# A gated linear recurrence and a gated linear unit on one core: another hand-written order of all queues, other PSUM banks, four groups of unread matmuls in place of eleven

## The chip, the cores and the metric

The kernel runs on one core of a Trainium2 chip. The metric is the device time of one execution in microseconds. All input and output tensors lie in HBM; the kernel is launched once.

## The reference

The input x has 4 sequences of 6336 steps with 256 channels, as have the two gates. A recurrence along time is computed for each channel, then a causal convolution of 5 taps whose sigmoid gates a linear map, then a second linear map.

```python
a_base = sigmoid(a_param)                        # 256 channels
log_a  = 8.0 * sigmoid(r_gate) * log(clip(a_base, 1e-6, 1 - 1e-6))
a_t    = exp(log_a)
x_gated = sqrt(maximum(1 - a_t * a_t, 1e-6)) * sigmoid(i_gate) * x
for t in range(S):
    h = a_t[:, t] * h + x_gated[:, t]
    y[:, t] = h
gate = sigmoid(causal_conv(y, conv_w))           # 5 taps, one set for each channel
out  = (gate * (y @ w_val)) @ w_out              # two 256 x 256 matrices
```

## The kernel before

The 25344 time steps (4 x 6336) are cut into 51 windows: two of 256 steps, 48 of 512 and a last one of 256. Windows are grouped into 28 chunks: chunks 0, 1, 2, 26 and 27 hold one window (0, 1, 2, 49 and 50), every other chunk holds two. Chunk 3 is windows 3 and 4, chunk 7 windows 11 and 12, chunk 16 windows 29 and 30, chunk 24 windows 45 and 46. The sequence boundaries fall inside chunks. All intermediate tensors live in rings of buffers that the work goes round: 4 windows each for r, i and x as they are loaded, 4 for the output, 3 for the gate, 5 chunks for a, 10 windows for u.

The program takes no decision at run time or by a scheduler. A text, `ORDER`, lists words, and a loop at L530 emits the instructions of each word in that order. Every engine takes its own instructions strictly in the order of the text, so the text fixes the queue of each engine and of SP, which issues all large DMAs. A word names an operation, its window or chunk, sometimes a half of the channels (0 or 1), and behind `@` the PSUM banks (of eight) that it writes. The framework adds semaphores where one instruction needs another's result or the buffer that it still reads. The operations of one window or chunk, in the order in which data passes through them:

| word | engine, line | what it does |
|---|---|---|
| `lr`, `li`, `lx` (window) | SP, L290 | loads 512 KB of r, i or x (256 KB for a short window) |
| `ta`, `tb` (chunk) | ACT, L308, L311 | tanh of r/2 and of i/2 (the sigmoids) |
| `tr` (chunk, half) | PE, L355 | transposes the tanh of r into PSUM, 16 matmuls for a pair of chunks |
| `ex` (chunk, half) | ACT, L376 | exp: a, for one chunk or a pair |
| `sq`, `sa` (chunk, half) | POOL, L384; ACT, L392 | a squared |
| `rt` (batch) | ACT, L403 | square root of 1 - a squared, for two or three chunks at once, with another activation table |
| `nt` (chunk) | PE, L418 | transposes the root back |
| `pp`, `up` (window) | POOL, L318, L330 | 1 + tanh, then times x |
| `xp`, `uv` (window) | PE, L335; DVE, L344 | the same product for windows 1, 2 and 6, with x passed through PSUM |
| `xg` (chunk) | DVE, L425 | times the root: the recurrence's input u |
| `xt` (chunk) | PE, L434 | transposes u |
| `sc` (chunk, half) | DVE, L456 | the scan along time |
| `cv` (window) | PE, L468 | the convolution, 20 matmuls with diagonal weights |
| `tg` (window) | ACT, L475 | tanh of half the convolution (the gate) |
| `vl` (window) | PE, L483 | y times w_val |
| `gv` (window) | DVE, L488 | (1 + gate) times val |
| `ou` (window) | PE, L498 | times w_out |
| `cd`, `ca` (window) | DVE, L506; ACT, L508 | copies the result out of PSUM |
| `st` (window) | SP, L519 | stores 512 KB |
| `wm` (number) | PE, L362 | five 128x512 matmuls of an identity into a bank that nobody reads |

The words `s_wl.0` to `s_wl.3` load the two weight matrices and `s_wcast` converts them on POOL. The loop at L530 puts in an activation table load (1.28 us each in the trace, at L535) whenever ACT goes from tanh or exp to the square root or back, so a run of `rt` costs two.

A load waits for the operation that frees its slot, and everything behind it in SP's queue waits too; a store waits for its copy in the same way. Words on PE wait likewise for the reader of the bank that they are going to write: `vl.44@2,3` waits for `tg.43`, for instance, where `cv.43` was the last to write banks 2 and 3.

```python
for word in ORDER.split():
    word, _, at = word.partition("@")
    name, *idx = word.split(".")
    if table.get(name, have) != have:
        have = table[name]
        nc.scalar.preload_act_table_set(have)
    emit[name](*[int(k) for k in idx], *[int(k) for k in at.split(",") if k])
```

Of the kernel before, what the change touches and what calls it, by code (L numbers as in the profile page):

```python
# [53 lines left out]
gv.9 st.7 cv.10@4,5 li.20 ta.12 li.18 sc.7.0 pp.16 li.17 vl.8@0,1 sq.10.0 vl.10@6,7 tg.10 lr.26 li.19 gv.8
ou.9.0@4,5 pp.13 gv.10 wm.2@2 ou.8.0@0,1 rt.5 up.14 cd.9.0 ou.10.0@6,7 tr.11.1@2 sc.7.1 st.9 up.16 lr.25 cd.10.0
cv.11@4,5 up.13 cd.8.0 st.10 nt.8@6,7 lr.23 tr.11.0@3 st.8 pp.15 xg.8 tg.11 vl.11@0,1 lr.24 lx.18 ex.11.1 up.15
xt.8@6,7 gv.11 lx.17 ex.11.0 nt.9@4,5 sc.8.0 sq.11.1 tb.10 cv.12@0,1 tr.12.0@3 xg.9 ex.12.0 li.22 pp.17 li.21 sc.8.1
tg.12 pp.18 ou.11.0@4,5 tb.11 xt.9@2,3 sq.11.0 vl.12@0,1 cd.11.0 cv.13@6,7 ta.14 sq.12.0 gv.12 st.11 li.23 cv.14@4,5
tg.13 sc.9.1 lr.29 pp.20 ou.12.0@0,1 ta.13 up.18 vl.13@6,7 cd.12.0 tr.12.1@3 tg.14 up.17 sc.9.0 st.12 tr.13.1@0,1
ex.12.1 lx.19 lx.20 nt.10@4,5 ex.13.1 li.24 sq.12.1 gv.13 tr.13.0@2,3 tb.12 xg.10 ou.13.0@6,7 sq.13.1 xt.10@4,5  # L60
cd.13.0 ex.13.0 cv.15@0,1 pp.22 sc.10.0 st.13 lx.21 cv.16@6,7 pp.19 lx.22 tg.15 lr.28 lr.30 sq.13.0 vl.15@2,3 tg.16
sc.10.1 li.25 vl.14@0,1 lr.27 pp.21 vl.16@6,7 gv.15 rt.6 sq.14.1 gv.14 ou.15.0@2,3 up.19 gv.16 cv.17@4,5 ou.14.0@0,1
cd.15.0 up.20 ou.16.0@6,7 cd.14.0 st.15 li.26 nt.11@2,3 cd.16.0 sq.14.0 lx.24 vl.17@0,1 tg.17 xg.11 st.14 lx.23
tb.13 st.16 gv.17 xt.11@2,3 up.21 cv.18@4,5 sc.11.1 sc.11.0 li.27 nt.12@0,1 li.28 ta.15 up.22 vl.18@6,7 tg.18 lr.32
pp.23 lr.31 ta.16 ou.17.0@4,5 pp.24 gv.18 up.24 tb.14 xg.12 tr.15.1@2,3 cv.20@6,7 cd.17.0 ex.15.1 xt.12@0,1 up.23
# [501 lines left out]
```

## Time and profile before

| what | before |
|---|---|
| device time, median of 3 runs | 290.36 us (290.32 to 290.96) |
| device time of the profiled execution | 290.72 us |
| its span, first to last instruction | 288.6 us |
| instructions in the span | 6363 |
| mean granted TensorE clock | 0.996 |
| moved by DMA | 104.76 MB, mean 363 GB/s |
| POOL products (L330) | 48, 100.9 us busy |
| DVE scans (L456) | 54, 105.8 us busy |
| PE convolutions (L468) | 1080 matmuls, 62.9 us busy |
| PE unread matmuls (L362) | 55, 14.0 us busy |

Times inside the span are counted from its start, in microseconds. Rows of the timeline give start and duration of instructions merged by line and shape, and in brackets the idle time of the engine before them and what ended it; rows of the waits give the total, the number and the longest of such waits. In the text, the time of a word is that of its instructions in the trace, found by counting through `ORDER` engine by engine.

### The profile page before, as it was taken

How to read it: one execution, taken by the hardware profiler on the slowest of the kernel's cores; microseconds unless marked ns; L12 is line 12 of the kernel's file. 1: busy time of each engine (PE TensorE's matmuls, PEld its weight loads, DVE VectorE, ACT ScalarE, POOL GpSimd, SP SyncE). 2: the span in 40 equal slices, each digit the busy share in tenths (PEclk: the TensorE clock that was granted, in tenths of full speed). 3: DMA queues.
4: the chain of work that ended last, by engine and by line, in shares of the span. 5: the costliest groups of instructions: out<-in, count | busy, mean ns of one | idle time of the engine just before them, and what ended most of it. 6: DMA issues, size and time to landing. Idle time of an engine off the chain costs nothing.

```text
span 288.6 us, 6363 instructions
## 1 busy us (share of the span) xinstructions
PE 250.6 (87%) x2552; PEld 169.4 (59%) x2552; DVE 247.0 (86%) x214; ACT 273.7 (95%) x197; POOL 241.5 (84%) x161
## 2 busy tenths in 40 slices
PE   2397799879898899889898999889799897999993
PEld 1253557547656677466567585467457664676552
DVE  5002899869999999999998999989999999999891
ACT  4999999999999999999999999999999999999754
POOL 1669469999999999999999999999998999496100
PEclk9999999999999999999999999999999999999998
DMA  7999999999999999999999999999999999885554
GB/s 240 396 392 409 407 374 385 357 385 371 403 407 410 410 395 366 375 346 417 418 408 341 376 413 414 418 395 396 351 352 412 420 386 408 263 292 208 199 221 182
DMA packets 29996, 104.76 MB, mean 363 GB/s; under 512 B 3335, under 2 KB 3854, under 8 KB 29966
## 3 DMA queue, kind: packets, MB, share of 16 engines
q1 hardware_dynamic: 29952, 104.35, 93.9%
q8 instruction: 20, 0.33, 0.5%
q14 instruction: 10, 0.08, 0.1%
q10 hardware_dynamic: 14, 0.01, 0.0%
HBM read 78.39 MB, written 25.95 MB: 362 GB/s over the span
## 4 chain that ended last, share of the span: by engine, by line
POOL 31%; PE 20%; DMA 15%; DVE 12%; ACT 12%; issue 7%; SPq 2%; DVEq 0%; ACTq 0%; POOLq 0%
POOL uring L330 14%; POOL ering L384 11%; DMA xring<-in_x_dram 8%; POOL tbring L318 6%; PE banks L468 6%; DMA iring<-in_i_gate_dram 6%; DVE yring L456 5%; DVE tgring L488 4%; PE banks L483 4%; PE banks L498 3%; PE banks L418 3%; ACT aring L376 3%; ACT tbring L311 3%; ACT ering L403 2%; SPq L290 2%
## 5 line engine op out<-in xcount | busy, mean ns | idle before, releaser
L330 POOL TENSOR_TENSOR uring<-tbring,xring 128x1024 bf16<-128x1024 bf16 (+1 forms) x48 | 100.9, 2116 | 11.1 <-DMA xring<-in_x_dram 10.6
L456 DVE TENSOR_TENSOR_SCAN yring<-aring,yring,banks 128x1024 bf16<-128x1024 f32 (+5 forms) x54 | 105.8, 1987 | 0.2
L384 POOL TENSOR_TENSOR ering<-aring 128x1024 f32<-128x1024 f32 (+2 forms) x54 | 91.7, 1715 | 14.7 <-ACT aring L376 14.6
L468 PE MATMUL banks<-yring,diag 64*64 64x512 bf16 (+7 forms) x1080 | 62.9, 361 | 4.6 <-DVE yring L456 3.6
L488 DVE SCALAR_TENSOR_TENSOR tgring<-tgring,banks 128x1024 bf16<-128x1024 bf16 (+1 forms) x51 | 59.3, 1178 | 5.1 <-PE banks L483 2.4
L498 PE MATMUL banks<-wo,tgring 128*128 128x256 bf16 x396 | 51.1, 274 | 7.5 <-DVE tgring L488 4.9
L376 ACT ACTIVATE aring<-banks,khf 128x2048 f32<-128x2048 bf16 (+3 forms) x38 | 53.9, 1467 | 0.4 <-PE banks L355 0.4
L475 ACT ACTIVATE tgring<-banks 128x1024 bf16<-128x1024 f32 (+1 forms) x51 | 50.5, 1007 | 3.0 <-PE banks L468 2.9
L318 POOL TENSOR_SCALAR tbring<-tbring 128x1024 bf16<-128x1024 bf16 (+1 forms) x48 | 49.0, 1030 | 4.4 <-ACT tbring L311 4.3
L498 PEld LDWEIGHTS <-tgring 128*128 128x128 bf16 x396 | 41.4, 114 | 18.6 <-DVE tgring L488 10.5
L483 PE MATMUL banks<-yring,wv 128*128 128x512 bf16 (+4 forms) x216 | 49.6, 361 | 1.6 <-ACT aring L376 0.8
L308 ACT ACTIVATE taring<-rring 128x2048 bf16<-128x2048 f32 (+2 forms) x28 | 47.6, 1718 | 2.4 <-DMA rring<-in_r_gate_dram 2.4
L311 ACT ACTIVATE tbring<-iring 128x2048 bf16<-128x2048 f32 (+2 forms) x28 | 47.9, 1719 | 0.0
L468 PEld LDWEIGHTS <-diag 64*64 64x64 bf16 x1080 | 29.1, 106 | 28.1 <-issue 11.6
L403 ACT ACTIVATE ering<-ering 128x4096 bf16<-128x4096 f32 (+5 forms) x15 | 44.7, 3016 | 0.1
L506 DVE COPY oring<-banks 128x1024 f32<-128x1024 f32 (+1 forms) x36 | 42.0, 1182 | 1.6 <-PE banks L498 1.1
L355 PE MATMUL banks<-ident_b,taring 128*128 128x128 bf16 x396 | 30.2, 230 | 9.4 <-ACT taring L308 7.2
L425 DVE TENSOR_TENSOR uring<-banks,uring 128x2048 bf16<-128x2048 bf16 (+2 forms) x28 | 30.4, 1093 | 6.7 <-PE banks L418 5.7
L355 PEld LDWEIGHTS <-taring 128*128 128x128 bf16 x396 | 26.1, 103 | 15.1 <-ACT taring L308 9.2
L483 PEld LDWEIGHTS <-wv 128*128 128x128 bf16 x216 | 19.9, 98 | 21.3 <-issue 7.1
L418 PE MATMUL banks<-ident,ering 128*128 128x128 f32 x198 | 29.7, 292 | 1.9 <-DVE yring L456 0.9
L418 PEld LDWEIGHTS banks<-ident,ering 128*128 128x128 f32 x198 | 25.9, 207 | 9.1 <-ACT ering L403 3.5
(45 smaller groups left out, 139.7 us busy)
## 6 DMA issues: line engine op xcount, KB each, us to landing
rring<-in_r_gate_dram SPq DMA_DIRECT2D x48, 512.0 KB, 7.9
iring<-in_i_gate_dram SPq DMA_DIRECT2D x48, 512.0 KB, 8.2
xring<-in_x_dram SPq DMA_DIRECT2D x48, 512.0 KB, 7.9
out_dram<-oring SPq DMA_DIRECT2D x48, 512.0 KB, 5.8
rring<-in_r_gate_dram SPq DMA_DIRECT2D x3, 256.0 KB, 4.4
iring<-in_i_gate_dram SPq DMA_DIRECT2D x3, 256.0 KB, 5.8
xring<-in_x_dram SPq DMA_DIRECT2D x3, 256.0 KB, 8.2
out_dram<-oring SPq DMA_DIRECT2D x3, 256.0 KB, 7.4
```

Of the source, the lines that this page charges most:

```text
L311: nc.scalar.activation(**tangent(c, tbring, NTI, iring, NII))
L318: nc.gpsimd.tensor_scalar(out=t, in0=t, scalar1=1.0, scalar2=1.0, op0=ALU.mult, op1=ALU.add)
L330: nc.gpsimd.tensor_tensor(out=u, in0=t1, in1=xt, op=ALU.mult)
L355: nc.tensor.transpose(out=bank[:, o:o + P], in_=taring[:, place(w, NTR), j, h * P:(h + 1) * P], identity=ident_b[:])
L376: nc.scalar.activation(out=dst, in_=src, func=ACT.Exp, scale=khf[:, h:h + 1], bias=khf[:, h:h + 1])
L384: nc.gpsimd.tensor_tensor(out=e, in0=a, in1=a, op=ALU.mult)
L418: nc.tensor.transpose(out=bank[:, k:k + P], in_=ering[:, e + q:e + wins[w] // 2:nq], identity=ident[:])
L456: nc.vector.tensor_tensor_scan(out=yring[:, h, col:col + o1 - o0], data0=aring[:, h, a_at[c] + o0:a_at[c] + o1], data1=xT[:, o0:o1], initi ...
L468: nc.tensor.matmul(out=gp[oh * 64:oh * 64 + 64, h, a:b], lhsT=diag[half * 64:half * 64 + 64, h, k, :], rhs=yring[half * 64:half * 64 + 64, ...
L483: nc.tensor.matmul(out=val[:, m, a:b], lhsT=wv[:, hk, m * P:(m + 1) * P], rhs=yring[:, hk, col:col + b - a], start=(hk == 0), stop=(hk == ...
L488: nc.vector.scalar_tensor_tensor(out=tgring[:, w % NTG, :, 0:wins[w]], in0=tgring[:, w % NTG, :, 0:wins[w]], scalar=1.0, in1=live.pop(("va ...
L498: nc.tensor.matmul(out=ops[:, j * D:(j + 1) * D], lhsT=gv[:, hk, j:wins[w]:J], rhs=wo[:, hk, :], start=(hk == 0), stop=(hk == H - 1))
```

## The change

Only the text `ORDER` is replaced; every function, ring, chunk and group of chunks stays as it was, and so do all line numbers. Both texts hold the same words except these: there are 11 `wm` words before and 4 after; and the copies of windows 5, 23, 34 and 39 go from ACT to DVE (`ca` to `cd`), those of windows 16, 29, 33 and 36 from DVE to ACT. The words stand in another order for every engine and for SP, and most PE words write other banks. The number of switches between activation tables is 18 in both.

In the head and around the places that are spoken of below, the diff reads:

```diff
 ORDER = """
-s_ident s_small s_kt s_diag lr.2 lr.0 s_wl.3 lr.1 li.0 lr.3 s_wl.2 ta.2 ta.0 lr.4 tr.0.1@0 ta.1 lr.6 tr.2.0@1 tb.0
-lr.5 tr.1.0@2 tr.0.0@3 tr.2.1@4 ex.2.0 li.1 tr.1.1@5 li.2 ex.1.1 li.3 ex.0.1 sq.1.1 lx.0 ex.1.0 li.4 sq.2.0 ex.0.0
-ex.2.1 sq.1.0 ta.3 sq.2.1 pp.0 sq.0.0 ta.4 sq.0.1 tb.1 lr.10 tr.3.0@4,5 tb.2 lr.9 lr.8 tr.3.1@2,3 lr.7 ex.3.0 lx.2
-s_wl.1 up.0 lx.1 ex.3.1 sq.3.0 lx.4 lx.3 wm.10@6 tb.3 sq.3.1 ta.6 pp.4 wm.5@6 wm.3@6 wm.9@6 wm.6@6 sq.4.1 lr.13 ta.5
...
-gv.9 st.7 cv.10@4,5 li.20 ta.12 li.18 sc.7.0 pp.16 li.17 vl.8@0,1 sq.10.0 vl.10@6,7 tg.10 lr.26 li.19 gv.8
...
-xt.8@6,7 gv.11 lx.17 ex.11.0 nt.9@4,5 sc.8.0 sq.11.1 tb.10 cv.12@0,1 tr.12.0@3 xg.9 ex.12.0 li.22 pp.17 li.21 sc.8.1
...
-sc.13.0 ou.19.0@4,5 pp.25 cd.19.0 up.25 wm.16@6 sc.13.1 st.19 li.32 nt.14@4,5 up.27 lx.29 li.31 ta.18 lr.36 lx.30
...
-xg.16 li.35 xt.15@4,5 sq.18.0 ca.23.0 gv.24 cv.26@2,3 li.36 ta.20 sc.15.0 sq.17.0 cv.25@6,7 st.22 tg.26 tr.19.0@0,1
...
-tr.25.1@0 up.42 ex.25.1 nt.22@4,5 cd.35.0 tg.38 ou.36.0@0,1 sq.24.0 xg.22 sa.25.1 st.35 tr.25.0@6 lr.50 vl.38@2,3
...
-vl.41@2,3 xg.24 ta.26 tr.27.0@6 xt.23@0,1 gv.41 ex.27.0 ou.39.0@4,5 tb.25 sc.23.0 cv.42@2,3 ca.39.0 ou.41.0@6,7
...
-sc.24.0 tr.27.1@7 ca.40.0 cv.44@0,1 ex.27.1 up.47 st.40 cv.43@2,3 ex.26.1 lx.49 sc.24.1 tg.44 sa.27.1 nt.25@6,7
-sq.26.1 tg.43 vl.42@0,1 sq.27.0 tb.26 xg.25 vl.44@2,3 sq.26.0 tb.27 vl.43@4,5 gv.42 pp.50 xt.25@6,7 pp.49 gv.44
-ou.42.0@0,1 rt.11 gv.43 ou.44.0@2,3 up.49 ca.42.0 sc.25.1 ou.43.0@4,5 ca.44.0 st.42 cv.45@0,1 ca.43.0 st.44
...
+s_ident s_small s_kt s_diag lr.0 s_wl.2 ta.0 lr.2 li.0 ta.2 tr.2.0@0 tr.0.1@1 lr.1 lr.3 lr.4 ta.1 lr.6 tb.0 lr.5
+ex.0.1 tr.1.1@2 ex.1.1 ex.2.0 tr.2.1@3 tr.1.0@4 ex.1.0 li.1 li.2 li.4 ex.2.1 ta.3 wm.6@5 tr.0.0@4 sq.2.0 ta.4 lx.0
+wm.9@5 li.3 lr.7 lr.10 lr.9 tr.3.1@2,3 tr.3.0@0,1 lx.1 lr.8 sq.2.1 pp.0 up.0 sq.1.0 ex.0.0 sq.0.0 lx.2 lx.3 xp.1@4
+s_wl.3 tb.2 lx.4 tb.1 ex.3.1 li.5 sq.3.1 lx.5 uv.1 s_wl.1 sq.0.1 sq.1.1 ex.3.0 tb.3 wm.11@5 ta.6 xp.2@4,5 ta.5 lr.13
+s_wl.0 rt.0 nt.0@0 sq.3.0 rt.2 rt.1 nt.2@1 uv.2 pp.4 sq.4.1 sq.4.0 xg.0 up.4 pp.3 xg.2 nt.1@2 xt.0@4,5 li.6 xg.1
+xt.1@2,3 tr.5.1@0,1 sc.0.0 up.3 s_wcast rt.3 sc.0.1 ex.5.1 nt.3@4,5 sc.1.1 sc.1.0 xg.3 cv.0@6,7 tg.0 lr.11 li.8
+xt.2@2,3 lr.14 li.7 lx.6 lr.12 sc.2.1 sc.2.0 cv.1@4,5 sq.6.1 vl.1@0,1 tr.5.0@6,7 vl.0@2,3 tg.1 tb.4 gv.1 gv.0
...
+nt.8@0,1 sc.7.0 cv.12@4,5 cd.8.0 xg.8 vl.12@6,7 tr.11.1@2 st.8 tg.12 lr.26 ex.11.1 ex.11.0 gv.12 xt.8@0,1 cv.11@4,5
...
+sc.14.0 cv.23@0,1 li.31 li.32 ou.22.0@2,3 cd.22.0 lx.30 ex.17.1 tb.16 nt.15@6,7 st.22 cv.25@4,5 lx.29 xg.15 ta.19
...
+pp.41 up.40 li.45 li.46 ex.23.1 sq.24.0 pp.42 xg.21 ou.34.0@2,3 xt.21@6,7 cv.37@0,1 gv.35 cd.34.0 ta.25 tr.25.1@2
...
+ex.26.1 cv.44@2,3 sc.24.1 sc.24.0 ex.27.0 ou.42.0@0,1 ex.27.1 tb.26 sq.26.0 pp.47 sq.27.0 sq.26.1 up.47 tg.44
+sa.27.1 ca.42.0 cv.43@6,7 tg.43 nt.25@2,3 xg.25 pp.49 st.41 st.40 vl.43@0,1 vl.44@6,7 st.42 gv.44 lx.49 li.50 lx.50
...
 """
```

More of the change, by code (lines that the diff above doesn't have):

```diff
@@ new lines @@
+ou.1.0@0 ou.0.0@1 ex.5.0 xt.3@2,3 cd.1.0 st.1 cd.0.0 ta.8 cv.2@4,5 tg.2 li.10 pp.5 st.0 sc.3.0 sc.3.1 vl.2@6,7
+xp.6@0,1 nt.4@4,5 ta.7 gv.2 uv.6 lx.7 up.5 lx.9 li.9 tb.5 lx.8 lr.15 tr.7.0@2,3 lr.17 tr.7.1@6,7 xg.4 ou.2.0@0,1
+sq.5.0 ex.7.0 xt.4@4,5 cd.2.0 sq.5.1 sq.6.0 sq.7.0 pp.7 sc.4.1 st.2 sc.4.0 ex.7.1 li.12 lr.16 tb.6 cv.3@2,3 cv.4@0,1
+tg.4 lr.18 li.14 lx.10 vl.4@6,7 gv.4 vl.3@0,1 tg.3 gv.3 sq.8.0 sq.7.1 rt.4 ou.4.0@6,7 pp.9 cd.4.0 cv.5@2,3
+ou.3.0@0,1 cv.6@6,7 cd.3.0 pp.8 up.8 up.7 tg.6 st.4 li.11 st.3 nt.5@0,1 tg.5 ta.9 vl.6@4,5 li.13 lx.11 lx.12 xg.5
@@ new lines @@
+lr.19 lr.20 gv.6 xt.5@0,1 sq.8.1 up.9 ta.10 vl.5@2,3 ou.6.0@4,5 nt.6@6,7 pp.10 up.10 sc.5.1 cd.6.0 tb.7 tr.9.1@4,5
+ex.9.1 gv.5 st.6 xg.6 sc.5.0 ou.5.0@2,3 tr.9.0@6,7 xt.6@4,5 pp.12 pp.11 lr.22 lr.21 tb.8 ex.9.0 cd.5.0 cv.7@0,1
+nt.7@2,3 tg.7 up.11 up.12 pp.13 li.15 sc.6.1 sc.6.0 wm.14@6 vl.7@0,1 cv.8@6,7 xg.7 st.5 ta.11 ta.12 gv.7 cv.9@4,5
+tg.8 tg.9 xt.7@2,3 sc.7.1 ou.7.0@0,1 lx.13 li.16 tb.9 sq.9.1 cv.10@6,7 vl.9@4,5 cd.7.0 tg.10 sq.9.0 vl.10@0,1 gv.9
+gv.10 sq.10.0 pp.14 ou.9.0@4,5 sq.10.1 cd.9.0 vl.8@6,7 lx.14 li.18 lx.16 lx.15 li.17 up.13 st.7 rt.5 ou.10.0@0,1
@@ new lines @@
+tb.12 gv.14 xg.10 cv.15@0,1 lr.27 pp.20 sq.12.1 pp.19 lx.20 lx.22 sq.13.1 ex.13.0 sq.13.0 st.11 lx.19 li.23 lr.30
+li.26 lr.28 xt.10@2,3 tg.15 up.19 pp.21 gv.13 lr.29 ou.13.0@4,5 vl.15@0,1 sc.10.0 up.20 sq.14.0 pp.22 cd.13.0
+ou.14.0@6,7 rt.6 gv.15 st.13 cd.14.0 li.24 cv.16@4,5 ou.15.0@0,1 tg.16 sc.10.1 cd.15.0 ta.15 nt.11@6,7 vl.16@2,3
+st.14 lx.21 xg.11 st.15 lr.31 lx.23 lr.32 lx.24 ta.16 gv.16 cv.18@0,1 xt.11@6,7 cv.17@4,5 vl.18@2,3 tg.18 up.22
+sq.14.1 up.21 sc.11.0 li.25 sc.11.1 tg.17 nt.12@0,1 tr.15.1@4,5 xg.12 tb.13 ex.15.1 tr.15.0@6,7 vl.17@0,1 pp.24
@@ new lines @@
+gv.18 ex.15.0 xt.12@2,3 pp.23 gv.17 li.27 li.28 lr.34 up.23 sq.15.1 up.24 ou.16.0@4,5 ca.16.0 ou.17.0@0,1 st.16
+sc.12.1 cd.17.0 cv.20@6,7 sq.16.1 cv.19@4,5 lx.26 st.17 ta.17 ou.18.0@0,1 lr.33 tg.20 sc.12.0 cd.18.0 tg.19 tb.14
+sq.16.0 vl.19@6,7 nt.13@4,5 vl.20@2,3 gv.19 st.18 gv.20 sq.15.0 cv.21@0,1 xg.13 tb.15 ou.19.0@6,7 vl.21@2,3 tg.21
+cd.19.0 lx.28 lx.25 xt.13@4,5 rt.7 pp.25 pp.26 gv.21 sc.13.1 up.26 ou.21.0@2,3 cv.22@6,7 ou.20.0@0,1 cd.21.0 st.19
+lx.27 sc.13.0 pp.27 up.25 li.30 li.29 nt.14@2,3 st.21 cv.24@4,5 cd.20.0 ta.18 xg.14 tg.24 lr.35 vl.24@0,1 tg.22
@@ new lines @@
+st.20 tr.17.0@2,3 lr.36 xt.14@4,5 pp.28 lr.37 lr.38 ex.17.0 up.27 up.28 tr.17.1@6,7 vl.22@2,3 gv.24 sc.14.1 gv.22
+sc.14.0 cv.23@0,1 li.31 li.32 ou.22.0@2,3 cd.22.0 lx.30 ex.17.1 tb.16 nt.15@6,7 st.22 cv.25@4,5 lx.29 xg.15 ta.19
+tg.23 sq.17.0 sq.18.0 lr.39 vl.23@2,3 lr.40 tg.25 xt.15@6,7 gv.23 ta.20 pp.30 cv.26@4,5 tb.17 sq.17.1 ou.23.0@2,3
+sq.18.1 tr.19.0@0,1 pp.29 sc.15.0 tg.26 li.33 li.34 up.30 tr.19.1@4,5 sc.15.1 cd.23.0 st.23 ex.19.0 lx.31
+ou.24.0@6,7 cd.24.0 nt.16@0,1 ex.19.1 up.29 ta.21 pp.32 xg.16 vl.25@2,3 cv.27@4,5 tg.27 sq.19.1 sq.19.0 st.24
@@ new lines @@
+xt.16@0,1 li.35 tb.18 pp.31 gv.25 ou.25.0@2,3 sc.16.1 cv.28@4,5 pp.34 sq.20.0 up.31 tg.28 lx.32 up.32 vl.28@6,7
+pp.33 cd.25.0 st.25 li.36 vl.26@4,5 vl.27@2,3 rt.8 lx.34 lr.41 lx.33 lr.42 gv.28 gv.26 ou.28.0@6,7 li.37 lx.35
+sq.20.1 ou.26.0@4,5 sc.16.0 cv.30@0,1 cd.28.0 cd.26.0 gv.27 nt.17@6,7 xg.17 tr.21.0@4 ou.27.0@2,3 cd.27.0 lx.36
+li.38 xt.17@6,7 lr.44 tb.19 lr.43 tr.21.1@5 tg.30 sc.17.0 sc.17.1 ex.21.0 ex.21.1 ta.22 pp.35 up.34 up.33 vl.29@2,3
+cv.29@0,1 nt.18@4,5 xg.18 tr.22.1@6 tr.22.0@7 li.39 li.40 tg.29 st.26 lx.37 ex.22.1 vl.30@0,1 xt.18@4,5 gv.29
@@ new lines @@
+cv.31@2,3 st.28 ex.22.0 lx.38 tb.20 tg.31 ou.29.0@6,7 pp.36 sq.21.0 ca.29.0 up.36 up.35 st.29 gv.30 cv.32@0,1
+ou.30.0@2,3 vl.32@6,7 tg.32 li.42 nt.19@0,1 st.27 ta.23 sc.18.1 sc.18.0 gv.32 sq.22.0 sq.21.1 vl.33@4,5 li.41
+sq.22.1 lx.39 lr.45 lr.46 cv.33@6,7 tb.21 xg.19 cd.30.0 xt.19@0,1 sc.19.0 pp.38 up.38 tg.33 pp.40 ou.32.0@2,3
+vl.31@6,7 cd.32.0 gv.31 gv.33 pp.37 st.32 lx.40 rt.9 cv.34@2,3 ou.31.0@6,7 st.30 sc.19.1 lr.47 lr.48 nt.20@4,5
+cd.31.0 up.37 tg.34 xg.20 vl.34@0,1 cv.35@2,3 gv.34 pp.39 lx.42 tb.22 xt.20@4,5 ou.33.0@6,7 cv.36@0,1 sc.20.1
@@ L101 @@
+cv.50@2,3 gv.49 ou.49.0@6,7 tg.50 vl.50@4,5 gv.50 ca.49.0 ou.50.0@4 ca.50.0 st.48 st.49 st.50
 """
```

66 lines of the change are left out of this document (16 added, 50 removed).

## The prediction

> **What bounds the kernel now.** I read the page first, its busy times, its slices and the first shares of its chain.
>
> ```profile
> PE 250.6 (87%) x2552; PEld 169.4 (59%) x2552; DVE 247.0 (86%) x214; ACT 273.7 (95%) x197; POOL 241.5 (84%) x161
> ...
> ACT  4999999999999999999999999999999999999754
> ...
> PEclk9999999999999999999999999999999999999998
> ```
>
> ACT is idle for 288.6 - 273.7 = 14.9 us only, nearly all of it in the first slice and the last three. The waits of ACT say where:
>
> ```profile
> ACT oring L508 <- PE banks L498: 3.9, 6, 1.0
> ACT tgring L475 <- PE banks L468: 2.9, 5, 1.4
> ACT taring L308 <- DMA rring<-in_r_gate_dram: 2.4, 4, 1.0
> ...
> ACT aring L376 <- PE banks L355: 0.4, 1, 0.4
> ```
>
> The first two rows (6.8 us) are almost all in the tail, and so are no loss of ACT's own: after 270 us PE sets the end. Between 7 and 270 us I find in ACT's timeline only three waits of over 0.25 us (0.32 for a load at 24, 0.38 for PE at 99, 0.32 at 194). So ACT's queue runs without a break up to the last tanhs, and the time of a word on ACT is the sum of the words ahead of it. Last I read the head and the tail in the timeline of ACT, with two rows of PE:
>
> ```profile
> 4.23 1.58 ACT L308 ACTIVATE taring<-rring 128x1024 bf16<-128x1024 f32 x2 [0.95 <-DMA rring<-in_r_gate_dram]
> 6.67 0.63 ACT L308 ACTIVATE taring<-rring 128x512 bf16<-128x512 f32 x1 [0.86 <-DMA rring<-in_r_gate_dram]
> 7.30 0.63 ACT L311 ACTIVATE tbring<-iring 128x512 bf16<-128x512 f32 x1
> ...
> 99.70 1.20 ACT L376 ACTIVATE aring<-banks,khf 128x1024 f32<-128x1024 bf16 x1 [0.38 <-PE banks L355]
> ...
> 258.86 1.03 ACT L475 ACTIVATE tgring<-banks 128x1024 bf16<-128x1024 f32 x1
> 259.80 1.58 ACT L311 ACTIVATE tbring<-iring 128x1024 bf16<-128x1024 f32 x2
> ...
> ```
>
> ```profile
> 259.19 2.75 PE L483 MATMUL banks<-yring,wv 128*128 128x512 bf16 x12
> ...
> 284.39 0.61 PE L498 MATMUL banks<-wo,tgring 128*128 128x256 bf16 x4 [0.85 <-DVE tgring L488]
> ```
>
> The tanh at 258.86 is tg.43. The twelve matmuls at 259.19 are vl.42, vl.44, vl.43; vl.44 writes banks 2 and 3, which tg.43 reads, and starts when it ends (259.19 + 0.87 = 260.06). From there PE has no gap until the 0.85 before its last word, ends at 285.00, and one copy and one store follow. So the end is: ACT's queue up to tg.43, then PE's queue behind vl.44.
>
> **The change part by part.** The sets of operations are equal but for seven of the eleven wm groups. Counted through both orders, ACT keeps 15 copies, two squares and 18 table loads, and no ACT group changes its count. So the order can give back only ACT's idle time and the tail.
>
> *The groups taken out.* In the row of 25 at 17.44 us (below) the first five take 2.34, the last five 1.24. Seven groups are 7 x 1.24 = 8.7 us of PE, each in a place where PE waits anyway: 0 on ACT, as long as the pace holds. In the head the cover is gone: without the five groups PE would have nothing to do from 17.65 (end of tr.3.1) to 25.48 (xp.2). The new order has wm.6 and wm.9 near 8 to 13 us, where PE waited 4.5 us for ta.3, and only xp.1 and wm.11 ahead of xp.2.
>
> ```profile
> 14.90 2.74 PE L355 MATMUL banks<-ident_b,taring 128*128 128x128 bf16 x24 [0.77 <-ACT taring L308]
> 17.44 6.77 PE L362 MATMUL banks<-ident_b 128*128 128x512 bf16 x25
> ...
> 27.27 1.06 PE L355 MATMUL banks<-ident_b,taring 128*128 128x128 bf16 x16
> ```
>
> Sixteen transposes are 1.06 us at 27 us and 24 are 2.74 (16 are 1.83) at 15 us: half pace costs 0.8 to 1.1 us a group of PE work. Behind the square roots of rt.3 stand tr.5.1, nt.3, cv.0, xt.2, cv.1 and then ACT's tg.1; ACT has there a table load and one exp (1.28 + 1.94 = 3.2 us) against 1.06 + 0.6 + 0.4 + 0.6 = 2.7 of PE's nt.3 to cv.1 at full pace. If nt.3 and xt.2 are slow it is about 1.4 more, less 0.5 cover; with tr.5.1 late too, 1.4 is lost. Bounds 0 and 1.4; I take 0.3, nearer the first, because PE has about 5 us of nearly unbroken work before cv.1, as long as it had from 14.9 to 19.8 before the pace rose.
>
> Here a rule of the Trainium skill speaks against the change. Its page "TensorE: Matmul & The Clock Gate", Part 1, says that about 3.4 us without work halve the array's clock and as long a busy stretch restores it. The 7.8 us hole would then be slow for certain, the sum 1.1 us longer. The trace agrees with a rise after sustained work (2.34 to 1.24); it shows no fall before the end, since the groups filled the holes.
>
> *The head.* Before, SP issues lr.2, lr.0, a weight, lr.1, li.0. After, it issues lr.0, a weight, lr.2, li.0, lr.1, so 256 KB of li.0 pass ahead of lr.1; and ta.1, which needs lr.1, still stands ahead of tb.0 on ACT. Before, ta.1 started at 6.67 when lr.1 landed, and tb.0 at 7.30 did not wait for li.0. After, the same bytes must land for ta.1 as had landed for tb.0: 7.30, or +0.63, and with nothing free behind it ACT carries that on. Bounds: 0, and 1.09 (262 KB at the first slice's 240 GB/s). A gain is excluded, since more bytes stand ahead. Starting ta.0 first gains nothing, since ta.1 waits at the end of both.
>
> *The middle.* At 99.70 ACT waited 0.38 for tr.12.0, which stood on PE behind nt.9 and cv.12. After, tr.12.1 and tr.12.0 stand ahead of nt.9: -0.38. Against it sc.7.0 goes on DVE from behind gv.9 to behind cd.10, so cv.12, tg.12 and the exps of chunk 11 follow it closely: sc.7.0 ends near 91.9 + 2.34 = 94.2, cv.12 at 95.5, while ACT arrives near 95.8. No wait, with 0.3 of room. Bounds -0.38 and +0.5; I take -0.38.
>
> *Loads and POOL.* lx.29 goes behind st.22, which waits on DVE's cd.22 (about 12 us later), while POOL's up.29 moves back by only 9.5 us of its queue. lr.39 and lr.40 stand behind. From issue to use the lead falls from 7.4 to about 4 us, against 7.9 from issue to landing (page, x loads): POOL may starve for up to 4 us. POOL's squares for rt.8 end about 5 us before ACT gets there. Later, sq.24.0 goes to the front of its group and waits for ex.23.0; behind it 14.5 us of POOL work lead to rt.10, with about 1 us of room where it was 1.8. Bounds on ACT 0 and 1.5; I take 0.3, as both places have room by these sums.
>
> *The tail.* On ACT tg.43 gets tb.26 and ca.42 in front of it: 0.96 + 0.91 = +1.87. On PE vl.43 and ou.42 go in front of vl.44, which leaves 0.86 + 0.87 = 1.73 us less behind it. Net +0.14. Bounds: -0.5, if PE's small gaps close, and +0.5. The words from cv.48 to ou.50 keep their order on PE.
>
> Sum: 0.63 + 0.3 - 0.38 + 0.3 + 0.14 = +1.0 us. On the profiled execution's 290.72 (span 288.6 and 2.1 around it) that is 291.7; its run lay 0.36 above the median of 290.36, so the forecast is 290.36 + 1.0 = 291.4.
>
> **The rivals.**
>
> *Waits cancel (no measurable change).* DMA's early rate, DVE's shuffles and the saved wait leave the head's 0.63 less the 0.38 and the tail's 0.14: +0.4, 290.8. For it: the same tail and the same ACT sums. Against: three more places where room is smaller.
>
> *TensorE goes slow in the head (slower).* The mechanism of the hole above, 1.4 in place of 0.3: +2.1, 292.5. For it: the 7.8 us hole. Against: PE is needed at full pace for only some 3 us there.
>
> *POOL late at the square roots (slower).* lx.29 or sq.24.0 costs 1.5 in place of 0.3, with rt.8 or rt.10 behind and the whole tail with it: +2.2, 292.6. For it: the shorter lead. Against: the 5 us and 1 us of room.
>
> *The tail gets shorter (faster).* If ACT reached tg.43 as early as before (258.9), PE's shorter rest would end it 1.7 us earlier: 288.6. It decides from the point where vl.44 starts before 260.06 + 0.87. For it: PE's rest is shorter by two words. Against: that needs 1.87 us of idle time on ACT ahead of tg.43, and from 7 to 258 us there is 1.0 in waits that a timeline shows.
>
> **How the numbers follow.** A measurement here can tell about 0.3% (0.87 us) from no change: 289.49 to 291.23. Forecast (+0.6 to +1.6) 0.39, of which 0.14 lies within that bound; cancelling 0.28, all within; slow pace 0.13; late POOL 0.10; shorter tail 0.10. That is faster 0.10, same 0.42, slower 0.48. The range goes from 289.9 (head's loss 0, tail -0.5) to 293.8 (both slower rivals together, +3.4); it leaves out the shorter tail and a pile-up of all the upper bounds (+5.0).
>
> **What the changed profile would show.** Head right: ta.1 (L308, 128x512, the second of its form) starts near 7.3, with a DMA wait of about 1 us before it. Pace: PEclk below 9 in a slice between 17 and 36 us, or L418 groups of eight at about 2 us, would favour the slow rival. Middle: no wait of L376 near 99 us. POOL: idle before L330 near 170 us, and ACT waiting before L403. Tail: tg.43 near 261.4 and ca.50 near 286.3; ACT's waits on L498 and L468 still about 6.8 us. Wrong would be: ACT's busy time other than 273.7, or waits of ACT in the middle of several us, or a vl.44 that starts before 260.9.

## The result, and the profile after

The changed kernel takes 292.34 us (median of 17 executions, 290.18 to 294.45) against 290.24 for the kernel before on the same chip (17 executions, 289.65 to 291.15): ratio 1.0071, 95% interval 1.0042 to 1.0099. So it is slower by 2.1 us, by more than the 0.3% that a measurement can tell. The spread has grown with the median, from 1.5 us to 4.3.

The profiled execution is one of the quickest of the changed kernel (290.48 us, span 288.7). It shows what the change does when nothing goes against it, and another one is needed for what it costs. First the page of this execution: busy times, ACT's slices, TensorE's granted clock.

```profile
PE 242.9 (84%) x2490; PEld 163.5 (57%) x2517; DVE 247.0 (86%) x214; ACT 273.2 (95%) x197; POOL 242.0 (84%) x161
...
ACT  4899999999999999999999999999999999999564
...
PEclk9995999999999999999999999999999999999999
```

ACT's busy time is what it was (273.2 against 273.7), and TensorE's has fallen by 7.7 us with the unread matmuls taken out. The new digit is the 5 in the fourth slice (21.7 to 28.9 us): the clock stood at half there. ACT's waits, in the columns of before:

```profile
ACT tgring L475 <- PE banks L468: 3.7, 3, 2.1
ACT taring L308 <- DMA rring<-in_r_gate_dram: 3.3, 4, 1.9
ACT oring L508 <- PE banks L498: 2.9, 5, 0.9
```

The tail's two rows are 6.6 us (6.8 before), the wait on L376 is gone, and the head's wait for r has gone from 2.4 to 3.3. The timeline of ACT has the head and the tail:

```profile
3.64 0.63 ACT L308 ACTIVATE taring<-rring 128x512 bf16<-128x512 f32 x1 [0.63 <-DMA rring<-in_r_gate_dram]
6.14 1.06 ACT L308 ACTIVATE taring<-rring 128x1024 bf16<-128x1024 f32 x1 [1.87 <-DMA rring<-in_r_gate_dram]
7.48 0.63 ACT L308 ACTIVATE taring<-rring 128x512 bf16<-128x512 f32 x1 [0.28 <-DMA rring<-in_r_gate_dram]
8.02 0.61 ACT L311 ACTIVATE tbring<-iring 128x512 bf16<-128x512 f32 x1
...
260.28 1.07 ACT L475 ACTIVATE tgring<-banks 128x1024 bf16<-128x1024 f32 x1
```

In order these are ta.0, ta.2, ta.1, tb.0 and tg.43. ta.1 has moved from 6.67 to 7.48; the long wait is now ta.2's, for lr.2. The timeline of PE in the head:

```profile
23.32 2.05 PE L335 MATMUL banks<-xring,ident 128*128 128x512 f32 x2 [6.22 <-DMA xring<-in_x_dram]
25.16 2.34 PE L362 MATMUL banks<-ident_b 128*128 128x512 bf16 x5
27.29 2.65 PE L335 MATMUL banks<-xring,ident 128*128 128x512 f32 x4
29.79 1.07 PE L418 MATMUL banks<-ident,ering 128*128 128x128 f32 x8
```

The hole behind tr.3 is there (6.22 us), a group of unread matmuls runs at half pace behind it (2.34), and the group of eight transposes at 29.79 is at full pace again (1.07). In this execution ACT has no wait of over 0.25 us between 14 and 270 us, and the last store starts 0.13 us earlier than in the profile of before.

### The profile page after: what moved, and what is told of

It is laid out like the page before. It is cut to its first block, busy times and chain, and to the rows that moved or that the text cites. A ratio compares the mean times of both kernels' runs of the same rounds, so it can differ in the third digit from the quotient of the medians.

```text
span 288.7 us, 6257 instructions
## 1 busy us (share of the span) xinstructions
PE 242.9 (84%) x2490; PEld 163.5 (57%) x2517; DVE 247.0 (86%) x214; ACT 273.2 (95%) x197; POOL 242.0 (84%) x161
## 4 chain that ended last, share of the span: by engine, by line
ACT 32%; PE 25%; DMA 17%; DVE 12%; issue 10%; SPq 2%; POOL 1%; ACTq 0%; DVEq 0%
DMA rring<-in_r_gate_dram 8%; ACT ering L403 7%; PE banks L468 7%; DVE yring L456 6%; ACT tgring L475 6%; ACT taring L308 5%; PE banks L498 5%; ACT aring L376 5%; PE banks L483 5%; DMA iring<-in_i_gate_dram 4%; ACT tbring L311 4%; PE banks L434 4%; ACT L535 3%; DMA xring<-in_x_dram 3%; DVE oring L506 3%
## 5 line engine op out<-in xcount | busy, mean ns | idle before, releaser
L376 ACT ACTIVATE aring<-banks,khf 128x2048 f32<-128x2048 bf16 (+3 forms) x38 | 53.8, 1472 | 0.1
L483 PE MATMUL banks<-yring,wv 128*128 128x512 bf16 (+7 forms) x189 | 48.8, 358 | 5.1 <-DVE yring L456 1.1
L355 PE MATMUL banks<-ident_b,taring 128*128 128x128 bf16 x396 | 27.8, 223 | 8.9 <-ACT taring L308 6.6
L355 PEld LDWEIGHTS <-taring 128*128 128x128 bf16 x396 | 24.4, 100 | 13.9 <-ACT taring L308 8.3
```

The costliest lines, as they stand in the source:

```text
L376: nc.scalar.activation(out=dst, in_=src, func=ACT.Exp, scale=khf[:, h:h + 1], bias=khf[:, h:h + 1])
L483: nc.tensor.matmul(out=val[:, m, a:b], lhsT=wv[:, hk, m * P:(m + 1) * P], rhs=yring[:, hk, col:col + b - a], start=(hk == 0), stop=(hk == ...
```

## The experiments

Ratios are to the kernel before on the same chip, with their 95% intervals. Differences in us between two runs are differences of their medians; the runs stood on several chips, on which the kernel before took 290.24 to 290.47. In the first four, theory A stands for the pace in the head, B for the pace in the middle, C for the loads.

**The changed kernel once more**, without an edit, for a second profile.

> The changed kernel as it is, for a second profile and more times. Its 17 times spread from 290.2 to 294.5 us, those of before only from 289.7 to 291.2, and its slow times go with a lower mean granted clock. Theory A (pace in the head): TensorE has nothing to do from 17.1 to 23.3 us, falls to half pace there, and comes back after one or two stretches of about 3.4 us, as it happens; times spread over some 4 us again, low times have a clock of 0.985 or more, and a profile of a slow time shows half pace well beyond 28.6 us with ACT waiting for PE between 30 and 45 us. Theory B (pace in the middle): half pace appears again somewhere between 50 and 270 us in slow times, with ACT waits there. Theory C (loads): the clock has nothing to do with it, and slow times show ACT or POOL waiting for DMA.

Measured: 292.31 us (290.59 to 294.98), ratio 1.0063 (1.0038 to 1.0089). The profiled execution has a span of 292.7 this time, 4.0 us more than the other's, and so it shows the loss. ACT's timeline in it has three waits in the middle that the first profile lacks:

```profile
84.82 1.91 ACT L311 ACTIVATE tbring<-iring 128x2048 bf16<-128x2048 f32 x1 [1.24 <-DMA iring<-in_i_gate_dram]
...
98.64 1.02 ACT L475 ACTIVATE tgring<-banks 128x1024 bf16<-128x1024 f32 x1 [1.14 <-PE banks L468]
100.99 2.30 ACT L376 ACTIVATE aring<-banks,khf 128x1024 f32<-128x1024 bf16 x2 [1.32 <-PE banks L355]
```

These are tb.9, tg.12 and ex.11.1: 3.7 us, and with 0.6 us in the head they make the 4.0 us by which the second profile ends later (some 0.2 is made up elsewhere). The chain of this execution (start, us, what) tells how they hang together:

```profile
76.46 8.20 DMA iring<-in_i_gate_dram
84.86 1.77 issue
...
88.95 5.34 ACT ering L403
94.33 1.98 PE banks L418 x8
96.32 2.28 PE banks L468 x17
```

The transfer is li.16, half of what tb.9 reads. tb.9 is late, so the square root rt.5 is late, and TensorE waits for it with nt.8. The PE timeline shows that wait, and nt.8 and cv.12 behind it at half pace (eight transposes were 1.07 above):

```profile
91.21 1.07 PE L498 MATMUL banks<-wo,tgring 128*128 128x256 bf16 x8 [0.58 <-DVE tgring L488]
94.33 1.98 PE L418 MATMUL banks<-ident,ering 128*128 128x128 f32 x8 [2.05 <-ACT ering L403]
96.25 2.35 PE L468 MATMUL banks<-yring,diag 64*64 64x512 bf16 x20
```

The trace's clock records have half pace from 93.6 to 100.5 us. Why li.16 is late is seen on SP. First the issue of li.16 and its use by tb.9 in the timelines of before:

```profile
66.20 0.33 SPq L290 DMA_DIRECT2D iring<-in_i_gate_dram  x1
...
78.99 1.94 ACT L311 ACTIVATE tbring<-iring 128x2048 bf16<-128x2048 f32 x1
```

Then the same in the first profile of after, with st.5 (L519) and lx.13 ahead:

```profile
75.02 0.34 SPq L519 DMA_DIRECT2D out_dram<-oring  x1
75.45 0.39 SPq L290 DMA_DIRECT2D xring<-in_x_dram  x1
75.89 0.86 SPq L290 DMA_DIRECT2D iring<-in_i_gate_dram  x1
...
82.93 1.91 ACT L311 ACTIVATE tbring<-iring 128x2048 bf16<-128x2048 f32 x1
```

Before, li.16 was issued at 66.20 and used at 78.99, 12.8 us later. After, tb.7, which frees its slot, comes 4.8 us later on ACT, and li.16 stands on SP behind st.5 and lx.13: issued at 75.89, wanted at 82.93, 7.0 us later. What a load takes there is the last line that the trace gives for L290 between 60 and 90 us, for before and for this second run:

```profile
DMA to landing us min/median/max: 5.9/7.4/8.6
```

```profile
DMA to landing us min/median/max: 6.3/7.7/10.1
```

A room of 7.0 us against a median of 7.4 to 7.7: ACT waits in one execution and not in the next.

**Five groups of unread matmuls back into the hole of the head.**

```diff
-... lx.2 lx.3 xp.1@4
+... lx.2 lx.3 wm.1@6 wm.2@6 wm.3@6 wm.4@6 wm.5@6 xp.1@4
```

> The changed kernel with five unread groups put back into TensorE's hole of 17.1 to 23.3 us, ahead of xp.1, and nothing else. Theory A: the clock stays full from about 12 us on, the spread shrinks to about 1 us, the median falls from 292.3 to 290.0 to 290.6. Theories B and C: the spread and the median stay, 292 or so.

Measured: 292.24 us (290.32 to 293.44), ratio 1.006 (1.0038 to 1.0083). PE's timeline shows the groups where they should be, and the hole closed:

```profile
17.43 5.56 PE L362 MATMUL banks<-ident_b 128*128 128x512 bf16 x25
23.82 1.10 PE L335 MATMUL banks<-xring,ident 128*128 128x512 f32 x2 [0.83 <-DMA xring<-in_x_dram]
```

xp.1 runs in 1.10 us in place of 2.05, and nothing is gained. The clock did not stay full, as theory A had expected: the slow stretch has moved to 32.1 to 35.6 us, over tr.5.1 and nt.3. ACT does not wait there either (its only wait of over 0.25 us between 15 and 270 us is the one below), so half pace in the head costs nothing in either place, and theory A falls. The profiled execution still waits 0.62 us at tb.9.

**The same, with lr.1 ahead of li.0.**

```diff
-... lr.0 s_wl.2 ta.0 lr.2 li.0 ta.2 tr.2.0@0 tr.0.1@1 lr.1 lr.3 ...
+... lr.0 s_wl.2 ta.0 lr.2 lr.1 ta.2 tr.2.0@0 tr.0.1@1 li.0 lr.3 ...
```

> The same with lr.1 issued ahead of li.0. By the head term of the forecast ta.1 starts near 6.7 in place of 7.48 and the whole queue of ACT comes 0.6 to 0.8 us earlier: 289.4 to 289.9 if a_head5 is at 290.2. If the head delay is absorbed later, no difference from a_head5.

Measured: 292.58 us (291.32 to 293.45), ratio 1.0067 (1.0044 to 1.009). In ACT's timeline ta.2 and ta.1 form one stretch that waits even longer for lr.2, and ta.1 does not come earlier:

```profile
7.14 1.57 ACT L308 ACTIVATE taring<-rring 128x1024 bf16<-128x1024 f32 x2 [3.00 <-DMA rring<-in_r_gate_dram]
```

So li.0 in front of lr.1 is not what holds the head up.

**The kernel before without the five groups of its head.**

```diff
-... lx.3 wm.10@6 tb.3 sq.3.1 ta.6 pp.4 wm.5@6 wm.3@6 wm.9@6 wm.6@6 sq.4.1 ...
+... lx.3 tb.3 sq.3.1 ta.6 pp.4 sq.4.1 ...
```

> The kernel before without its five unread groups of the head (wm.10, 5, 3, 9, 6); TensorE then has nothing from 17.6 to 25.5 us. Theory A: it becomes like the changed kernel, median 1.5 to 3 us longer than before, spread of several us, mean clock 0.97 to 0.985. Theories B and C: 290.2 to 290.5 with the narrow spread of before.

Measured: 292.63 us (291.03 to 293.47), ratio 1.0063 (1.004 to 1.0086). PE's timeline shows half pace behind the hole (sixteen transposes of L355 were 1.06 us at 27.27 in the kernel before):

```profile
25.44 3.75 PE L335 MATMUL banks<-xring,ident 128*128 128x512 f32 x4 [7.38 <-DMA xring<-in_x_dram]
28.99 1.91 PE L355 MATMUL banks<-ident_b,taring 128*128 128x128 bf16 x16
```

The mean clocks do not tell it: theory A's 0.97 to 0.985 came in two of the six executions (0.985), the others have 0.998 or more. The first clock record in this trace is the rise to full pace at 31.4 us, and the time ahead of the first record counts as full in the mean. In the kernel before that rise is at 19.9, in the changed kernel at 11.8. So the mean clock leaves out the first slow stretch, and in the head it cannot be compared between two orders.

ACT's timeline shows two new waits behind the square roots:

```profile
38.03 2.06 ACT L376 ACTIVATE aring<-banks,khf 128x2048 f32<-128x2048 bf16 x1 [1.72 <-PE banks L355]
...
41.30 0.60 ACT L475 ACTIVATE tgring<-banks 128x512 bf16<-128x512 f32 x1 [0.72 <-PE banks L468]
```

In the order of before the groups are worth some 2 us (2.2 by the medians, 1.8 by the ratio), at ex.5.1 and tg.1. In the changed order ACT passes the same stretch without these waits, and TensorE is back at full pace at 28.8 us there, not at 31.4. So this price belongs to an order and not to the hole.

Three theories went into the next four runs: H (the head's loads), L (li.16), M (TensorE's pace in the middle).

**The head's loads and tanhs in the order of before.**

```diff
-... lr.0 s_wl.2 ta.0 lr.2 li.0 ta.2 tr.2.0@0 tr.0.1@1 lr.1 lr.3 lr.4 ta.1 lr.6 ...
+... lr.2 lr.0 lr.1 li.0 lr.3 s_wl.2 ta.2 ta.0 lr.4 tr.2.0@0 tr.0.1@1 ta.1 lr.6 ...
```

> The changed kernel with only its first five loads and ScalarE's first two tanh passes put back in the order of before (lr.2 ahead of lr.0 and both ahead of lr.1, then li.0; ta.2 ahead of ta.0). Three theories are compared in these four runs. H, the head loads: in the changed kernel ta.2 waits 1.9 to 3.0 us for lr.2 to land, lr.6 goes into ta.2's slot and so is issued 1.5 us later, and ScalarE enters its long stretch 0.7 to 1.3 us late. L, one load in the middle: li.16 is issued 10 us later than before (behind st.5), so that tb.9 waits for it by 0 to 1.2 us near 83 us. M, the pace in the middle: TensorE stands still 2 to 3 us near 90 to 94 us and drops to half pace for 6.8 us in some executions, where ScalarE then waits 2.5 us for tg.12 and ex.11.1. H expects here ta.1 at 6.6 to 6.9 us, rt.0 near 27.3, and a median 0.7 to 1.2 us below the changed kernel's: 291.1 to 291.6. L expects tb.9 to wait as much more as the head is earlier, and the median to stay at 292.3. M expects 292.0 to 292.5 with clocks spread from 0.97 to 0.99 as in the changed kernel.

Measured: 290.93 us (288.79 to 292.57), ratio 1.0006 (0.9985 to 1.0028): 1.4 us less than the changed kernel. The wait of tb.9 is there in its profile (1.02 us), and the spread stays wide. In this profile ta.1 starts as late as 7.84; the later profiles with this order have ta.1 at 5.8, 5.8 and 6.5, so the first transfers vary by 2 us from one execution to the next.

**li.16 directly behind li.15, ahead of st.5 and lx.13.**

```diff
-... pp.13 li.15 sc.6.1 ... xg.7 st.5 ... ou.7.0@0,1 lx.13 li.16 tb.9 ...
+... pp.13 li.15 li.16 sc.6.1 ... xg.7 st.5 ... ou.7.0@0,1 lx.13 tb.9 ...
```

> The changed kernel with one load moved: li.16 directly behind li.15 on SP's queue, ahead of st.5 and lx.13, which issues it some 4 us earlier (its slot comes free with tb.7 near 71 us). L expects no wait of ScalarE ahead of tb.9, 0 to 1.2 us less there and as much less ahead of rt.5, so that nt.8's hole on TensorE is no shorter in itself, and a median 0.6 to 1.2 us lower: 291.1 to 291.7. If the late load is also what tips TensorE into the slow pace near 94 us (L and M in a row), the clock of all timed executions is near 0.988 (the head's one slow stretch alone), and the median comes to 290.3 to 290.8. H and M alone expect 292.0 to 292.5.

Measured: 290.81 us (289.98 to 291.91), ratio 1.0008 (0.9991 to 1.0025): 1.5 us less than the changed kernel, from one word. SP's timeline has li.15 and li.16 together, and ACT's has tb.9 without a wait:

```profile
71.13 1.65 SPq L290 DMA_DIRECT2D iring<-in_i_gate_dram  x2
```

```profile
82.76 1.95 ACT L311 ACTIVATE tbring<-iring 128x2048 bf16<-128x2048 f32 x1
```

The room is now 10.5 us (72.26 to 82.76). L holds. The part of its expectation that all clocks would then be near 0.988 does not: six of the twelve executions are at 0.982 or less.

**Two groups of unread matmuls near 90 us.** The bank is not a free one, as the expectation has it: they write bank 2, which still holds transposed inputs of chunk 7, so that this chunk is scanned over other numbers.

```diff
-... st.9 ou.8.0@6,7 ... lx.17 nt.8@0,1 sc.7.0 ...
+... st.9 wm.2@2 ou.8.0@6,7 ... lx.17 wm.3@2 nt.8@0,1 sc.7.0 ...
```

> The changed kernel with two groups of unread matmuls (five of 512 columns each) put back near 90 us: one ahead of ou.8.0, one ahead of nt.8, both into a free bank. M expects no half pace near 94 us in any execution, clocks near 0.988 throughout, tg.12 and ex.11.1 without waits, and a median 1.5 to 2 us lower than the changed kernel's: 290.3 to 290.8. L and H expect no gain: 292.0 to 292.5, or up to 0.5 us above the changed kernel where the second group holds nt.8 up.

Measured: 292.62 us (291.45 to 293.51), ratio 1.0063 (1.0038 to 1.0089). In PE's timeline the hole ahead of nt.8 has shrunk to 0.18 us and nt.8 is at full pace, but cv.12 then waits for DVE's scan (sc.7.0), and the scan, in DVE's timeline, for the groups themselves (L362), since they write the bank that it reads:

```profile
94.09 1.23 PE L418 MATMUL banks<-ident,ering 128*128 128x128 f32 x8 [0.18 <-ACT ering L403]
96.35 1.27 PE L468 MATMUL banks<-yring,diag 64*64 64x512 bf16 x20 [1.02 <-DVE yring L456]
```

```profile
93.95 2.35 DVE L456 TENSOR_TENSOR_SCAN yring<-aring,yring,banks 128x1024 bf16<-128x1024 f32 x1 [1.70 <-PE banks L362]
```

In ACT's timeline tg.12 and ex.11.1 wait all the same, 0.79 in place of 2.46:

```profile
97.67 1.02 ACT L475 ACTIVATE tgring<-banks 128x1024 bf16<-128x1024 f32 x1 [0.41 <-PE banks L468]
99.08 2.30 ACT L376 ACTIVATE aring<-banks,khf 128x1024 f32<-128x1024 bf16 x2 [0.38 <-PE banks L355]
```

So this run puts a wait of its own where it takes one away. It neither shows nor refutes that the pace there has a price: M stays untested by it.

**All three, with the five groups of the head.** (Chunk 7 as above.)

> All three at once, with the five groups of unread matmuls ahead of xp.1 that an earlier run tried. If H, L and M each hold a part and nothing else is lost, the median comes to 288.8 to 290.0, below the kernel before, with clocks of 0.99 or more. If the loss of the changed kernel sits at other places (loads later in the span, the queue of POOL, the tail), it stays at 291.5 to 292.5.

Measured: 290.99 us (290.65 to 292.34), ratio 1.0024 (1.0007 to 1.004). tb.9 does not wait, but the groups near 90 us hold up the scan as before, and with it tg.12 by 1.27 and ex.11.1 by 0.38 us. So they were left out of the next runs.

**Both edits to loads, and nothing else** (the diffs of the head and of li.16 together).

> The changed kernel with both edits to loads and nothing else: the head's loads and ta.2 in the order of before, and li.16 directly behind li.15. Each alone took 1.4 to 1.5 us off the changed kernel's 292.3. If the two losses stand one behind the other on ScalarE (H and L both), they add, and the median comes to 289.2 to 290.0, at or below the kernel before, with no wait ahead of tb.9 and a spread under 2 us. If they are one loss (an earlier head only lets tb.9 wait longer, and the other way round), it stays at 290.7 to 291.0. Clocks are expected at 0.975 to 0.988, as in the changed kernel, without a price.

Measured: 290.08 us (288.95 to 292.19), ratio to before 0.9992 (0.997 to 1.0015): 2.3 us less than the changed kernel, no different from before by this measurement. The two losses add for the most part (1.4 and 1.5 alone), a bit less than expected. ACT's waits in its profile:

```profile
ACT tgring L475 <- PE banks L468: 3.7, 3, 2.1
ACT oring L508 <- PE banks L498: 2.9, 5, 0.9
ACT taring L308 <- DMA rring<-in_r_gate_dram: 1.7, 2, 1.2
...
ACT tbring L311 <- DMA iring<-in_i_gate_dram: 0.6, 1, 0.6
```

The tail is that of the changed kernel to the tenth; what has gone is half of the wait for r in the head. The last row is tb.0's, at 7 us, not tb.9's.

**The same, with the five groups of the head.**

> The same, with the five groups of unread matmuls ahead of xp.1. If the slow pace at 20 to 29 us has a price of its own, this is 0.5 to 1.5 us under the run without the groups; if the two paces do not matter in this order, as the earlier run with the groups says, it is within 0.4 us of it, with clocks of 0.99 and more.

Measured: 290.18 us (288.81 to 291.69), ratio 0.9996 (0.9976 to 1.0017), all clocks at 0.985 or more. Its profile has full pace from 20.9 to 287 us, so for all the work behind the square roots too, and nothing is gained: the pace in the head has no price in this order, a second time.

**The kernel before with li.16 late.**

```diff
-... ta.9 li.16 up.9 ... st.5 tr.9.1@4,5 lr.20 ...
+... ta.9 up.9 ... st.5 li.16 tr.9.1@4,5 lr.20 ...
```

> The kernel before, with li.16 alone moved back on SP's queue, behind st.5 and ahead of lr.20: it is issued near 73.6 us instead of 66.0. L expects it to land some 8 us later, near 81.6, so that tb.9, which starts at 78.8 now, waits 2 to 3.6 us, and that all of ScalarE behind it is late by that much: median 292.3 to 294.0. If the loads are hidden (the rivals' view, a load has ten us to spare), nothing changes: 290.2 to 290.6.

Measured: 292.58 us (291.18 to 293.87), ratio 1.0072 (1.0045 to 1.01): 2.1 us for one load. On SP it is issued at 73.66, and ACT's timeline has

```profile
80.66 1.91 ACT L311 ACTIVATE tbring<-iring 128x2048 bf16<-128x2048 f32 x1 [1.68 <-DMA iring<-in_i_gate_dram]
```

so it landed after 7.0 us, a bit earlier than I had said. From there to its end this profile is 1.5 us behind the profile of before: the wait is passed on nearly whole.

**The kernel before with the head's loads in the changed order.**

```diff
-... lr.2 lr.0 s_wl.3 lr.1 li.0 lr.3 s_wl.2 ta.2 ta.0 lr.4 ...
+... lr.0 lr.2 s_wl.3 li.0 lr.1 lr.3 s_wl.2 ta.0 ta.2 lr.4 ...
```

> The kernel before, with the head's loads and tanh passes in the order of the change: lr.0, lr.2, li.0, lr.1 (the small weight load stays third) and ta.0 ahead of ta.2. H expects ta.2 to wait some 2 us for lr.2, ta.1 0.8 to 1.3 us later, rt.0 0.7 to 1.2 us later, and most of it at the end: median 290.9 to 291.5. If the head's delay is made up later, 290.2 to 290.6.

Measured: 290.31 us (289.62 to 291.06), ratio 0.9992 (0.9978 to 1.0005). Nothing is lost, and theory H as I had put it fails here. ACT's timeline in it:

```profile
5.09 1.06 ACT L308 ACTIVATE taring<-rring 128x1024 bf16<-128x1024 f32 x1 [1.02 <-DMA rring<-in_r_gate_dram]
6.60 0.63 ACT L308 ACTIVATE taring<-rring 128x512 bf16<-128x512 f32 x1 [0.45 <-DMA rring<-in_r_gate_dram]
```

ta.2 runs 1.05 us earlier than in the changed kernel. What this run does not have is the weight load between lr.0 and lr.2, as SP's timeline of the changed kernel shows it (L268 is s_wl.2):

```profile
0.72 0.39 SPq L290 DMA_DIRECT2D rring<-in_r_gate_dram  x1
1.16 0.56 SPq L268 DMA_DIRECT2D oring<-in_moe_w_out_dram  x1
1.77 0.57 SPq L290 DMA_DIRECT2D rring<-in_r_gate_dram  x1
```

That weight load puts lr.2 back by 0.6 us of issue and by its own bytes. It is the likeliest cause of what the head loses; moving it alone was not tried, so that stays argued.

## Why the prediction was right, and where it was wrong

The forecast was 291.4 us with 289.9 to 293.8 and slower as the likeliest sign; the median is 292.34. The sign and the frame (ACT's queue without free time, so any wait is kept to the end) held. The loss was put at 1.0 us and is 2.1. That the median lies inside the range is in part luck, since two of the five terms of the sum (head, loads) stood for steps that cost nothing while other steps, close by, cost more. One of the prediction's own signs of being wrong, waits of ACT of several us in the middle, is absent from the first profile and present in the second (3.7 us). The ends of the range do not quite follow from the terms either: these give 290.1 and 293.7.

*Groups taken out, 0.* Right in the first profile: no wait of ACT replaces them. The condition was that the pace holds, and in the second profile it does not hold near 94 us.

*Pace in the head, +0.3 (0 to 1.4).* The hole came (6.2 us), and the clock fell to half at 22.0 us. The Trainium skill says this, in "TensorE: Matmul & The Clock Gate", Part 1, of about 3.4 us without work. The price was 0: 292.24 with the hole filled against 292.3, and 290.18 against 290.08. The rival "TensorE goes slow in the head" had its mechanism right and its price wrong. The reason for which I took a low value (PE is needed at full pace for some 3 us only) held for the changed order, and b_nohead shows that the rival's price is real in the other one.

*Head, +0.63.* ta.1 moved by 0.81 and 1.32 us in the two profiles; 0.7 (with li.16 in place, where the intervals overlap) to 1.4 us of the median hang on this order. The profiles say the same more weakly: rt.0 starts at 27.9 to 28.9 us in the six with the changed head, at 27.0 to 28.5 in the four with the head of before. The size was fair and the step was wrong: I let li.0 pass lr.1, but li.0 and lr.1 exchanged changes nothing in either kernel, and it is ta.2 that waits, for lr.2. "Starting ta.0 first gains nothing" was right.

*Middle, -0.38.* Right: in the first profile the wait at 99 us is gone, the one of 0.32 at 194 too; from rt.4 to the tail ACT gains 0.72. "No wait, with 0.3 of room" behind sc.7.0 was right there and no more than that: in the second profile ACT comes to tg.12 later and still waits 1.14 us there and 1.32 at ex.11.1, after nt.8 and cv.12 at half pace. The upper bound (+0.5) was too low for it.

*Loads and POOL, +0.3 (0 to 1.5).* This is the step that failed. I worked out lx.29 and sq.24.0, and neither costs anything: POOL waits 0.33 us near 171 and 2.79 at sq.24.0, and ACT never waits at a square root. (lx.29's lead is 6.3 us and not 4, as up.29 moved back by 11.8 us and not by 9.5.) The load that costs 0.9 (with the head's loads put back) to 1.5 us is li.16 behind st.5, whose room fell from 12.8 to 7.0 us; put back in the same way, it costs the kernel before 2.1. The same sum that I made for lx.29 (lead from issue to use against the median landing) would have shown it, had I made it for every load that is moved back.

*Tail, +0.14.* From tg.43, less the 1.87 of the two words put in front, to the last copy three profiles of this order lose 0.31 us: a bit more than said, well inside the bounds. tg.43 came at 260.28, not 261.4 (the terms give 261.6), since the first profile had no loss in the middle.

So the first profile ends 0.13 us ahead of before: +0.27 from the head at rt.4, -0.72 in the middle, +0.31 in the tail. With the two load edits what is left of the change is 290.08 against 290.44, 0.4 us less, inside the bound. The median of the changed kernel lies 2.1 us above before because most executions have something on top: of the profiles of the changed order with li.16 late, five of six wait 0.62 to 1.24 us at tb.9; with it moved, none of four does.

What stays open is the part of TensorE's pace in the spread. Over the 29 executions of the changed kernel those with a mean clock of 0.984 or more have a median of 290.65 (10), the others 292.98 (19). With li.16 moved the two groups are 290.62 and 291.10 (six each). The loads have their price at clocks alike: the two kernels with the groups in the head and li.16 late have 16 executions at 0.985 to 0.997 and a median of 292.35, and both load edits with the same groups give 290.18 at 0.985 to 0.999. But there, too, the executions of lower clock are the longer ones: in the last kernel the five at 0.990 or less have a median of 291.39, the seven above 289.59.

A slow stretch in the middle can cost by itself. In the profile of the run with the head's loads alone put back, the clock is at half from 188.4 to 191.8 us, and ACT waits for PE (timelines of PE and ACT):

```profile
188.14 1.88 PE L418 MATMUL banks<-ident,ering 128*128 128x128 f32 x8 [0.51 <-ACT ering L403]
```

```profile
192.30 1.02 ACT L475 ACTIVATE tgring<-banks 128x1024 bf16<-128x1024 f32 x1 [1.00 <-PE banks L498]
```

No wait of ACT over 0.25 us stands between tb.9 and this one. In the first profile and in that of both load edits the same eight transposes take 1.23 us, behind a hole of the same length (0.50 and 0.51), and ACT does not wait there. Near 94 us the late tb.9 and the slow stretch come together in the second profile, but three others in which tb.9 waits 0.62 to 1.18 us kept their pace there. So no run here tells how much of the spread the pace makes, and how much of that follows from the late load.

## What to carry to other kernels

In a queue that has no free time, check every load that an order moves back: its room from issue to use against what a load takes there, its slowest as well as its median. When a median moves and the profile does not, take a second profile and look at its waits; a room close to the landing time is a coin that falls anew in each execution. A filler for the clock is worth what the work right behind the hole needs, so its price found in one order says nothing about another.

## What the hardware showed that I had not expected

Loads of one size (512 KB) in one stretch (60 to 90 us, where the DMA engines are busy for 90% or more of every slice) take 4.4 to 10.3 us from issue to landing over six profiles of the changed order, in the kernel before 5.9 to 8.6. In the first 8 us the same order of loads lets ta.1 start anywhere from 5.8 to 7.8 us.

TensorE's clock fell and rose in steps of 3.41 us: half from 22.0 to 28.8 in the first profile, 32.1 to 35.6 with the groups in the head, 93.6 to 100.5 in the second profile. The fall at 93.6 came though TensorE had worked for 1.5 of the 3.4 us before it (0.4 of tr.11.0, 1.07 of ou.8.0), so a wholly idle stretch is not needed. The fall at 188.4 above came behind 1.72 us of work in 3.41, the one at 32.1 behind 1.73. In the first profile TensorE worked 2.3 of the 3.4 us up to 93.7, and its pace held.

The kernel before, with its eleven groups, had a mean clock of 0.995 or more in every execution beside these runs; the changed one had 0.968 to 0.988. Both means count the start as full, where the trace has no clock record yet, though 24 transposes at 14.90 took 2.74 us there in the kernel before.
